# Attention masks of three batches moved from TensorE products to compare-and-multiply on VectorE

## The chip, the cores and the metric

The kernel runs on one core of one Trainium2 chip. The metric is the device time of one execution in microseconds (us); lower is better. The engines are named as in the profile: PE is TensorE's matmul, PEld its weight load, DVE is VectorE, ACT is ScalarE, POOL is GpSimd, SP issues transfers.

## The reference

Four batches, eight heads, 768 positions, head size 64. Every query and key is given to one of 16 clusters of its head; a query sees only keys of its own cluster. The result goes through a two-layer MLP with ELU.

```python
q_assign = np.argmax(np.einsum('bhsd,hcd->bhsc', q_n, c_n), axis=-1)
k_assign = np.argmax(np.einsum('bhsd,hcd->bhsc', k_n, c_n), axis=-1)
mask = q_assign[:, :, :, None] == k_assign[:, :, None, :]
scores = scale * np.matmul(q, k.transpose(0, 1, 3, 2))
scores = np.where(mask, scores, -1000000000.0)
scores = scores - np.max(scores, axis=-1, keepdims=True)
attn = np.exp(scores)
attn = attn / (np.sum(attn, axis=-1, keepdims=True) + 1e-09)
# attn @ v, then x of (3072, 512):
h = x @ w_in                                   # (512, 2048)
g = np.where(h > 0.0, h, alpha * (np.exp(np.minimum(h, 0.0)) - 1.0))
return (g @ w_out).astype(np.float32)          # (2048, 512)
```

## The kernel before

The work is cut into 48 blocks, `n` from 0 to 47. A block is one batch, one third of the queries (256 of them) and one pair of heads; `blocks` runs over batches, then thirds, then the four pairs. So a batch has twelve blocks.

`scores(n)` makes the scores of one block with the keys on the partitions. Three score tiles `s` of 128x1024 (two heads, two key tiles of 128, 256 queries) are filled in PSUM. For each key tile there is a pair of float32 products over the 64 numbers of a head (L402, the two heads on the two halves of the partitions) and a pair of bf16 products that add the mask (L411). For the mask, `hot` holds for every position a one-hot vector over the 16 clusters of the heads, with the heads on the partitions, and `qm` holds plus or minus a very large number by the query's cluster, made by `masks(n)` on ACT (L376, two instructions). Masked scores get a hugely negative term, and the exponential (L419, ACT) makes them 0 in the SBUF tile `p`. There is no maximum taken off.

`sums(n)` adds the three `p` tiles on DVE (L425 to L427), from block 10 on. `values(n)` multiplies `p` with `v` into the PSUM bank `o_bank` (L448) and makes the row sums with a product by ones into a tile `d` (L437). ACT copies both out (L462, L464), DVE takes the reciprocal (L465), POOL scales (L466). `check(n)` reads the reciprocal once more on ACT (L472).

`hidden` makes four columns' tiles of the MLP's inner layer (L487), ACT, POOL and DVE make the ELU of it (L497, L498, L504, L506, L508); the DVE part of one `hidden`, called `elu`, is issued behind the next one's products, and holds its PSUM tile until then. `outer` is the second layer: seven products (L517) into `o_bank` and `f_bank` in turn, with sums and differences of their parts on DVE and POOL (L548 to L584), so that each of the two banks is emptied before a later product writes it again.

PSUM has these two banks and a pool of three tiles `banks` of two banks each, shared by score tiles, `d`, `hidden`, transposes and similarities. `p` has three tiles.

The order is written out by hand, and every engine runs its instructions in that order. In the loop over `n` it is: `values(n-1)`, loads, `masks(n+1)`, `scores(n)`, `check(n-1)`, `sums(n)`, in blocks 8 to 11 of a batch the transposes of the next batch's q and k (L312, DVE), and then one group of MLP steps. A third's MLP has four groups, one a block: two `hidden`; two `hidden`; four products; three products. The group lies `LAG = 7` blocks behind the attention of its third, so that a batch's blocks 3, 7 and 11 have the first kind.

At a batch's last block the next batch's clusters are made between the MLP steps: `similar` multiplies with the centroids (L333) and transposes on DVE (L340); `assign` finds the largest of 16 and makes `oh` and `hot` (L350, L352, L362), and copies `hot` with its halves exchanged (L365), which the mask products of half of the heads need. The query's are behind the first `hidden`, the key's and `masks` of the next block behind the second:

```python
beside.append(None)
for j in range(2):
    beside.append(lambda b=b, j=j: [similar(b + 1, j, half) for half in range(2)])
    beside.append(lambda b=b, j=j: [assign(b + 1, j, half) for half in range(2)])
beside.append(lambda n=n: masks(n + 1))
```

In the first 176 us the MLP's weights, which arrive as 64-bit numbers, are decoded on DVE, ACT and POOL (L246 to L265), a few between the score tiles.

## Time and profile before

| | |
|---|---|
| median of 3 runs | 1054.38 us (1052.81 to 1054.87) |
| profiled execution | 1053.93 us, its span 1051.9 us |
| PE clock granted | 0.991 |
| PE busy | 1009.7 us, 96% of the span |
| DVE busy | 531.3 us, 51% |
| ACT busy | 343.2 us, 33% |
| POOL busy | 182.2 us, 17% |
| from 24 to 175 us | PE 128.58 busy, DVE 146.38 of 151.00 |
| from 467 to 710 us, twelve blocks later in the run | PE 241.57 busy, DVE 112.61 of 243.00 |

The busy time of an engine is the time in which at least one of its instructions was being worked on. PE's records overlap, so what one product costs is read from the start of one to the start of the next. In the timeline a row is the start, the duration, the engine, the line, the operation with its tiles and shapes, how many equal ones it holds, and in brackets the idle time ahead of it with what ended it. All times count from the start of the span.

### The profile page before, as it was taken

What the parts mean: (1) busy time and instruction counts of PE and PEld (TensorE: products, weight loads), DVE (VectorE), ACT (ScalarE), POOL (GpSimd) and SP (SyncE); (2) the same over time, 40 slices, a digit from 0 to 9 for tenths busy, and PEclk for the clock granted to TensorE, in tenths of its full rate; (3) what the DMA queues carried; (4) which work ended last, traced back from release to release, by engine and by line L of the source; (5) the groups of instructions that cost most, each with busy time, mean ns of one, the idle gap of its engine ahead of it and who ended that gap; (6) DMA issues with size and microseconds to landing.
All of it is one profiled execution on the core that took longest, in us unless ns stands there. A gap on an engine that the chain in (4) does not pass through costs nothing.

```text
span 1051.9 us, 14992 instructions
## 1 busy us (share of the span) xinstructions
PE 1009.7 (96%) x6403; PEld 785.7 (75%) x6403; DVE 531.3 (51%) x638; ACT 343.2 (33%) x595; POOL 182.2 (17%) x193
## 2 busy tenths in 40 slices
PE   6978997999999999999999999999999999999996
PEld 4545775778778778778877877877887787788885
DVE  4999996484344246375335325456423433433131
ACT  4665540332332242233234234223323323421010
POOL 0466654111011011011011011011011011011010
PEclk9999998999999999999999999999999999999999
DMA  9628331100122103210014012210010010100000
GB/s 306 237 89 195 107 86 31 51 16 16 50 43 49 40 27 60 51 31 17 16 45 77 20 37 59 46 36 26 21 36 17 30 36 16 31 21 1 21 1 23
DMA packets 103961, 55.60 MB, mean 53 GB/s; under 512 B 83408, under 2 KB 96720, under 8 KB 103888
## 3 DMA queue, kind: packets, MB, share of 16 engines
q1 hardware_dynamic: 103888, 54.57, 19.2%
q8 instruction: 52, 0.85, 0.4%
q14 instruction: 21, 0.17, 0.1%
HBM read 48.27 MB, written 6.29 MB: 52 GB/s over the span
## 4 chain that ended last, share of the span: by engine, by line
PE 82%; DVE 14%; ACT 2%; issue 1%; POOL 1%; DMA 0%; ACTq 0%; DVEq 0%; POOLq 0%
PE banks L487 29%; PE f_bank L517 16%; PE o_bank L517 12%; PE o_bank L448 10%; PE banks L402 9%; DVE ex L261 4%; DVE ex L246 2%; PE banks L437 2%; PE banks L411 2%; DVE r L465 1%; DVE w_out L249 1%; DVE w_in L249 1%; ACT qm L376 1%; PE banks L333 1%; ACT p L419 1%; PE banks L322 1%
## 5 line engine op out<-in xcount | busy, mean ns | idle before, releaser
L487 PE MATMUL banks<-xT,w_in 128*128 128x256 f32 x1536 | 338.4, 381 | 0.9 <-ACT p L419 0.6
L487 PEld LDWEIGHTS banks<-xT,w_in 128*128 128x128 f32 x1536 | 290.6, 190 | 47.7 <-issue 4.2
L402 PE MATMUL banks<-qT,kT 64*128 64x256 f32 x1152 | 168.2, 392 | 4.9 <-ACT p L419 4.4
L448 PE MATMUL o_bank<-p,v_raw 128*64 128x256 f32 x1152 | 144.3, 385 | 11.0 <-ACT p L419 11.0
L419 ACT ACTIVATE p<-banks 128x1024 f32<-128x1024 f32 x144 | 140.6, 1022 | 13.3 <-PE banks L411 11.8
L465 DVE RECIPROCAL r<-r 128x256 f32<-128x256 f32 x48 | 84.0, 1750 | 116.1 <-ACT r L464 116.0
L497 ACT ACTIVATE gT<-banks 128x1024 f32<-128x1024 f32 x48 | 49.1, 1023 | 277.9 <-PE banks L487 277.9
L504 DVE SCALAR_TENSOR_TENSOR gT<-gT,banks 128x1024 f32<-128x1024 f32 x48 | 58.4, 1216 | 155.1 <-POOL gT L498 155.0
L402 PEld LDWEIGHTS banks<-qT,kT 64*128 64x128 f32 x1152 | 88.7, 189 | 55.2 <-PE o_bank L448 11.1
L448 PEld LDWEIGHTS o_bank<-p,v_raw 128*64 128x64 f32 x1152 | 77.9, 137 | 64.4 <-ACT p L419 15.4
L498 POOL TENSOR_SCALAR gT<-gT 128x1024 f32<-128x1024 f32 x48 | 50.2, 1046 | 313.3 <-ACT gT L497 313.0
L466 POOL TENSOR_TENSOR xT<-xT,r 128x256 f32<-128x256 f32 x48 | 40.7, 847 | 324.5 <-DVE r L465 324.4
L517 PE MATMUL o_bank<-w_out,gT 128*128 128x256 f32 x384 | 90.7, 390 | 6.3 <-POOL w_out L298 6.3
L462 ACT COPY xT<-o_bank 128x256 f32<-128x256 f32 x48 | 17.7, 369 | 218.0 <-PE o_bank L448 218.0
L517 PEld LDWEIGHTS o_bank<-w_out,gT 128*128 128x128 f32 x384 | 73.6, 194 | 20.1 <-POOL w_out L298 7.3
L517 PE MATMUL f_bank<-w_out,gT 128*128 128x256 f32 x384 | 87.1, 380 | 1.5 <-POOL w_out L252 1.5
L411 PE MATMUL banks<-qm,hot 64*128 64x256 bf16 x576 | 80.5, 271 | 2.0 <-DVE hot L362 2.0
L517 PEld LDWEIGHTS f_bank<-w_out,gT 128*128 128x128 f32 x384 | 73.1, 191 | 11.6 <-POOL w_out L252 1.9
L425 DVE TENSOR_TENSOR psum<-p 128x1024 f32<-128x1024 f32 x38 | 46.6, 1226 | 42.2 <-ACT p L419 42.2
L376 ACT ACTIVATE qm<-hot,minus,big 64x256 bf16<-64x256 bf16 x96 | 56.7, 591 | 4.1 <-DVE hot L362 3.3
L426 DVE TENSOR_TENSOR psum<-psum,p 128x1024 f32<-128x1024 f32 x38 | 46.9, 1235 | 6.0 <-ACT p L419 3.0
L517 PE MATMUL f_bank<-w_sum,g_sum 128*128 128x256 f32 x192 | 44.7, 386 | 1.2 <-DVE part L564 1.2
(109 smaller groups left out, 859.4 us busy)
## 6 DMA issues: line engine op xcount, KB each, us to landing
v_raw<-in_v_dram SPq DMA_DIRECT2D x48, 384.0 KB, 3.2
w_sum<-in_moe_w_out_dram SPq DMA_DIRECT2D x12, 512.0 KB, 3.7
out_dram<-o_sb SPq DMA_DIRECT2D x24, 256.0 KB, 2.0
q_raw<-in_q_dram SPq DMA_DIRECT2D x48, 96.0 KB, 3.7
k_raw<-in_k_dram SPq DMA_DIRECT2D x48, 96.0 KB, 3.3
w_sum<-in_moe_w_in_dram SPq DMA_DIRECT2D x8, 512.0 KB, 6.9
w_out<-in_moe_w_in_dram SPq DMA_DIRECT2D x8, 512.0 KB, 10.2
w_out<-in_moe_w_out_dram SPq DMA_DIRECT2D x4, 512.0 KB, 4.2
```

The lines of the kernel that those rows point to most:

```text
L376: nc.scalar.activation(qm[n][rows], hot[b, 0][rows, side(pr, e), ts(third, QS)], Act.Identity, scale=m, bias=minus[rows, pr % 2 : pr % 2 + 1],
L402: nc.tensor.matmul(s[:, e, ts(m, QS)], lhsT=T[i, 1][rows, ts(kt, P)], rhs=T[i, 0][rows, cols], start=True, stop=False,)
L411: nc.tensor.matmul(s[:, e, ts(m, QS)], lhsT=hot[b, 1][rows, side(pr, e), ts(kt, P)], rhs=qm[n][rows], start=False, stop=True,)
L419: nc.scalar.activation(p, s, Act.Exp, scale=SCALE)
L426: nc.vector.tensor_tensor(to, to, pu[n, 2], op=Alu.add)
L448: nc.tensor.matmul(o_bank[64 * e : 64 * e + 64, :QS], lhsT=raw["v", n][:, e, kt], rhs=p[:, e, ts(m, QS)], start=(kt == 0), stop=(kt == NT ...
L465: nc.vector.reciprocal(r, r)
L487: nc.tensor.matmul(hf[:, f], lhsT=w_in[:, ch, ts(4 * n + f, P)], rhs=xT[b, third][:, ch], start=(ch == 0 and f % 2 == 0), stop=(ch == KC - 1),
L497: nc.scalar.activation(t, hf, Act.Exp)
L498: nc.gpsimd.tensor_scalar(t, t, 1.0, 0.0, op0=Alu.min, op1=Alu.max)
L504: nc.vector.scalar_tensor_tensor(t, t, -1.0, hf, op0=Alu.add, op1=Alu.max)
L517: nc.tensor.matmul(to[:, :QS], lhsT=left[:, f], rhs=right[:, f], start=(f == 0), stop=(f == FC // 2 - 1),)
```

## The change

In batches 2 to 4 (`b > 0`) the scores get no mask products and no `qm`. The exponential makes `p` of all scores, and behind it DVE masks `p` in place: twelve instructions a block compare the query's cluster number with the key's and multiply `p` by the outcome. `qc` holds the query's numbers as bytes, the same on every partition, for eight heads and the 256 queries of a third; `kc` holds the key's numbers, one per partition, for each key tile and head. Both are made on PE from `hot` by a product with `index16`, the number of each one-hot row, and copied out of PSUM by ACT: `key_numbers` once a batch, `query_numbers` once a third, in the place of `masks`. Batch 1 stays as it was. The one-hot `hot` has no exchanged half in batches 2 to 4; the tiles of `hot`, `oh` and `qm` share places with others or have one buffer fewer.

```diff
+    numbers = const.tile([P, NC], F32, name="numbers")
+    for n in range(NC):
+        nc.gpsimd.memset(numbers[:, n : n + 1], float(n))
+    sq = work.tile([P, H, NC], F32, name="sq", tag="r", bufs=1)
+    index = const.tile([P, H], F32, name="index")
+    nc.vector.tensor_tensor(
+        sq,
+        ident.rearrange("q (h c) -> q h c", c=NC),
+        numbers.unsqueeze(1).to_broadcast([P, H, NC]),
+        op=Alu.mult,
+    )
+    nc.vector.tensor_reduce(index, sq, axis=Axis.X, op=Alu.add)
+    index16 = const.tile([P, H], BF16, name="index16")
+    nc.vector.tensor_copy(index16, index)
...
-            hot[b, j] = route.tile([P, 2, S], BF16, name="hot", tag=f"hot{j}", bufs=1 + j)
+            hot[b, j] = route.tile([P, 2 if b == 0 else 1, S], BF16, name="hot", tag=f"hot{j}", bufs=1)
...
-        oh = route.tile([P, HS], BF16, name="oh", tag="oh", bufs=1)
+        oh = work.tile([P, HS], BF16, name="oh", tag="r", bufs=1)
...
-        for e in range(2):
+        for e in range(2 if b == 0 else 0):
             at = 64 * e
             nc.vector.tensor_copy(h[64 - at : 128 - at, 1, cols], h[at : at + 64, 0, cols])
...
+    def key_numbers(b):
+
+        ps = banks()[:, 0]
+        kc[b] = route.tile([P, NT, H], F32, name="kc", tag="kc", bufs=2)
+        for kt in range(NT):
+            nc.tensor.matmul(
+                ps[:, ts(kt, H)], lhsT=hot[b, 1][:, 0, ts(kt, P)], rhs=index16, start=True, stop=True
+            )
+        nc.scalar.copy(kc[b].rearrange("p t h -> p (t h)"), ps[:, : NT * H])
+
+    def query_numbers(b, third):
+
+        to = qc[b, third] = route.tile([P, H, QS], U8, name="qc", tag="qc", bufs=2)
+        ps = [banks() for _ in range(2)]
+        for e in range(2):
+            for pr in range(NPR):
+                rows = slice(32 * pr, 32 * pr + 32)
+                nc.tensor.matmul(
+                    ps[pr // 2][:, pr % 2, ts(e, QS)],
+                    lhsT=index16[rows, 2 * pr + e : 2 * pr + e + 1].to_broadcast([32, P]),
+                    rhs=hot[b, 0][rows, 0, ts(third, QS)],
+                    start=True,
+                    stop=True,
+                )
+        for half in range(2):
+            nc.scalar.copy(
+                to[:, 4 * half : 4 * half + 4],
+                ps[half].rearrange("p a (e n) -> p (a e) n", e=2),
+            )
+
     def masks(n):
         b, third, pr = blocks[n]
-        qm[n] = route.tile([P, QS], BF16, name="qm", tag="qm", bufs=2)
+        if b > 0:
+            if pr == 0:
+                query_numbers(b, third)
+            return
+        qm[n] = route.tile([P, QS], BF16, name="qm", tag="qc", bufs=2)
...
-                        stop=False,
+                        stop=b > 0,
                     )
-                for e in range(2):
+                for e in range(2 if b == 0 else 0):
...
             nc.scalar.activation(p, s, Act.Exp, scale=SCALE)
+            for e in range(2 if b > 0 else 0):
+                for m in range(2):
+                    nc.vector.scalar_tensor_tensor(
+                        p[:, e, ts(m, QS)],
+                        qc[b, third][:, 2 * pr + e],
+                        kc[b][:, 2 * u + m, 2 * pr + e : 2 * pr + e + 1],
+                        p[:, e, ts(m, QS)],
+                        op0=Alu.is_equal,
+                        op1=Alu.mult,
+                    )
...
+            beside.append(lambda b=b: key_numbers(b + 1))
             beside.append(lambda n=n: masks(n + 1))
```

## The prediction

> **What bounds the kernel now.** I read the page's busy shares first, then its chain, then the timeline of one block at a time. The first two say that TensorE (PE) sets the end, the third says by what step.

> ```profile
> PE 1009.7 (96%) x6403; PEld 785.7 (75%) x6403; DVE 531.3 (51%) x638; ACT 343.2 (33%) x595; POOL 182.2 (17%) x193
> PE 82%; DVE 14%; ACT 2%; issue 1%; POOL 1%; DMA 0%; ACTq 0%; DVEq 0%; POOLq 0%
> L411 PE MATMUL banks<-qm,hot 64*128 64x256 bf16 x576 | 80.5, 271 | 2.0 <-DVE hot L362 2.0
> ```

> The chain's 14% of VectorE (DVE) lies in its first 176 us, where the weights are decoded. The change puts no mask there: its masks begin with batch 2, at 467 us. From 176 us on PE follows PE. The L411 row is a trap: 80.5 us busy for 576 mask products looks like 60 us in the three batches concerned. The timeline gives their real step. This is PE in one block, which I call a D block (its MLP group holds the last three products):

> ```profile
> 511.91 0.60 PE L437 MATMUL banks<-psum,ones 128*64 128x256 f32 x4
> 512.45 0.70 PE L402 MATMUL banks<-qT,kT 64*128 64x256 f32 x4
> 512.98 0.28 PE L411 MATMUL banks<-qm,hot 64*128 64x256 bf16 x2
> 513.09 0.60 PE L402 MATMUL banks<-qT,kT 64*128 64x256 f32 x4
> 513.53 0.28 PE L411 MATMUL banks<-qm,hot 64*128 64x256 bf16 x2
> ...
> 515.90 3.72 PE L517 MATMUL f_bank<-w_sum,g_sum 128*128 128x256 f32 x16
> 519.46 3.62 PE L517 MATMUL o_bank<-w_sum,gT 128*128 128x256 f32 x16
> 522.91 3.62 PE L517 MATMUL f_bank<-w_out,gT 128*128 128x256 f32 x16
> ```

> From start to start a score pair takes 0.44 us and a mask pair 0.11 (512.98 to 513.09). VectorE in the same block:

> ```profile
> 513.13 1.75 DVE L465 RECIPROCAL r<-r 128x256 f32<-128x256 f32 x1 [3.25 <-ACT r L464]
> 516.19 1.23 DVE L425 TENSOR_TENSOR psum<-p 128x1024 f32<-128x1024 f32 x1 [1.30 <-ACT p L419]
> 517.52 1.23 DVE L426 TENSOR_TENSOR psum<-psum,p 128x1024 f32<-128x1024 f32 x1
> 518.77 0.69 DVE L427 TENSOR_TENSOR psum<-psum 128x512 f32<-128x512 f32 x1
> 519.66 0.42 DVE L570 TENSOR_TENSOR o_sb<-f_bank,part 128x256 f32<-128x256 f32 x1 [0.20 <-PE f_bank L517]
> ```

> L570 empties f_bank, and the third product (522.91) writes f_bank again: L570 has only 2.8 us to spare. VectorE is half idle, but its order is fixed, and this is the place where that counts.

> [...] L554 at 582.32 is recorded with 0.42 us, and L555 behind it starts at 582.66, 0.34 later. [...] L300 took 3.24 us beside POOL's L298, where the equal L299 took 1.23. [...]

> **The change, part by part.** V is the start of a block's row sums (L437). Before, the MLP group starts at V+3.99 in kinds A, C and D (529.10 to 533.09, 571.06 to 575.05, 511.91 to 515.90) and at V+4.66 in B (549.74 to 554.40). MLP groups: A hidden 0 and 1, B hidden 2 and 3, C four products, D three. Batches 2 to 4 have 36 blocks: three first ones (n = 12, 24, 36), six other B, and nine each of C, D and A.

> 1. Mask products gone. Six pairs of 0.11: 0.65 us a block, so the group starts at V+3.35. In B one bank pair is held by a pending elu; only two go round, and the third score tile waits for the first exponential (before: 0.40 us idle at 553.12). L376, 2 x 0.6 us on ScalarE (ACT), stood ahead of that exponential and is gone: score tile 3 can start at V+2.55, the group at V+3.6. Gain 1.05 in B. Six B: +6.3; nine C: +5.85; nine D: +5.85; three A without new products (n = 23, 35, 47): +1.95.

> 2. Masks on VectorE: 12 a block, 432 in all, 128x256 with a per-partition scalar. The trace has no such row. Below, 0.34 (the step above); above, 0.42, the whole recorded time of a 256-element instruction, no overlap. The pointer may add: L191 (64 elements, with pointer) took 251 ns, L178 (without) 224. I take 0.38. They stand behind the reciprocal, whose end also releases POOL's L466 (723 ns at least, reads SBUF): once a block it locks out a mask for about 0.7. Masks therefore take 12x0.38+0.7 = 5.3 us, V+2.95 to V+8.2. VectorE's total, 531 us and 432x0.38 = 164, stays far below the span; only its lateness counts.
>    - D: the sums take 3.27 (516.19 to 519.46) and end at V+11.5, L570 behind them (0.42) at V+11.9. The third product wants f_bank at V+10.35: 3.35, and 3.55 and 3.45 for the two products ahead of it. Stall 1.55, in seven D blocks; in two (n = 22, 34) the transposes L312 (1.83) stand between too: 3.4. Sum 17.7.
>    - C: an elu delays the reciprocal's end to V+3.2; sums, L549 (1.14) and L554 (0.34) then free f_bank at V+13.25, the fourth product wants it at V+13.8 (three products of 3.45 behind V+3.35): hidden. With transposes (n = 21, 33) V+15.1: 1.3 each, 2.6.
>    - A at n = 23, 35: masks, sums and transposes hold VectorE until V+13.3, then L340 (0.58) empties the query's first similarity at V+13.9. Hidden 1 needs that bank and would be ready at V+11.9 (3.35, hidden 0 of 7.1, similarities of 1.43): 2.0 each, 4.1 for both.
>    - B: elu follows at V+13.4; hidden 3 ends only at V+17.6, and its bank comes from an exponential. Hidden; without that cover the C block's first scores would wait.

> 3. Key numbers, three times, behind the key's similarities. Before, PE went on with L448 at once (467.19), and VectorE's last transposes of hot came 4 us later:

> ```profile
> 465.76 1.50 PE L333 MATMUL banks<-kT,cT 128*32 128x384 f32 x16
> 467.19 2.81 PE L448 MATMUL o_bank<-p,v_raw 128*64 128x256 f32 x24
> 471.33 0.58 DVE L362 STREAM_TRANSPOSE hot<-oh 128x384 bf16<-128x384 bf16 x1
> ```

>    Now PE waits for that transpose. Without one half's copies (L365, 0.54) it ends at 471.25; six small products, the copy of kc, which the second query bank waits for, and eight query products end at about 472.25: values 5.05 late. Behind PE's wait are values, row sums and scores. The scores then run as in B, without the present stall: 1.05 back. Net 4.0 each, 12.0. Not shown in the trace: small products, from nothing to 0.1 each (a 64x128 bf16 weight load is 95 ns).

> 4. Query numbers ahead of six A blocks (n = 15, 19, 27, 31, 39, 43). PE's eight products, at most 8 x 0.11, hide under ACT's reading of the row sums (until V+1.18). Then ACT copies twice 128x1024 (as L497: 1.02). Score tiles 2 and 3 wait for those copies, the third until V+3.25; the group starts at V+4.25. Loss 0.25 each, 1.5. If bytes are written more slowly or quickly, 0 to 0.6 each.

> 5. Prologue: 16 memsets on POOL (L919's stand 0.035 apart, L216 takes 0.10: 0.6 to 1.6 together), then three instructions on VectorE ahead of cen, 0.29+0.29+0.16. The chain runs through cen (0.75 to 5.66): loss 0.8, from 0 to 1.7. The shared tags of oh, qc and hot cost nothing: their last readers end blocks earlier, and the second oh is behind the first on the same engine. No DMA is added, and SP's queue keeps its order.

> Sum: gains 6.3+5.85+5.85+1.95 = 19.95; losses 17.7+2.6+4.1+12.0+1.5+0.8 = 38.7. Net 18.7 slower. The profiled execution took 1053.93 us (span 1051.9); that gives 1072.6. The median of three, 1054.38, is 0.45 above it.

> **Rivals.**
> - Cheap masks: 0.34 each and no lock. D then stalls 0.34 seven times and 2.2 twice (6.8), C 0.2, L340 1.7: 3 slower, 1057. For it: POOL gets its 0.7 in an idle gap today. Against: the gap (1.30) is filled.
> - Faster: the D wait vanishes. It decides at 12 masks by V+6.3, which with the lock means 0.25 us a mask. Then only step 3, 4 and 5 remain against 19.95: 5.65 faster, 1048.3. Against: below the shortest 256-element step in the trace.
> - Full serial masks at 0.44 or above: D 2.3 and 4.1, C late in all blocks, L340 2.8: about 30 slower, 1083. For it: in-place writes; against: no wait stands between the four of a tile in the built order.
> - The change does not do what it says: nothing gained on PE, if mask pairs ran beside the scores all along. The 0.54 steps of 0.44 + 0.11 speak against it; it would give 1090.

> **How the numbers follow.** Forecast 0.72, cheap masks 0.13, faster 0.05, serial masks or no gain 0.10. A measurement of this kernel tells 0.2% (2.1 us) from no change. Faster by more: 0.06, with a tail of the cheap case. Within: 0.06, the cheap case with a short key wait. Slower: 0.88. The forecast's own bounds are 0.34 to 0.42 a mask (6 either way) and 1 us on each key wait: 1062 to 1083. Reaching for the cheap case and a part of the serial one: 1056 to 1086.

> **What would show it.** L411 down to 144 pieces; PE gaps at the third D product released by L570, about 1.5 us; a gap of 4 us behind L333 released by hot, three times; mask rows with starts 0.38 apart and one hole of 0.7; POOL L466 longer than 0.73. It is wrong if the third D product starts without a gap, if the key gap is below 2 us, or if masks start under 0.3 apart.

## The result, and the profile after

The changed kernel takes 1082.33 us (median of four runs, 1079.81 to 1083.55), against 1054.43 for the kernel before beside it: a ratio of 1.0264, 95% interval 1.0242 to 1.0287. The profiled execution took 1081.51 us, of which 1078.0 are its span; the forecast was 1072.6, with a range from 1056 to 1086. The direction was right, and the size was short by 9 to 10 us.

Busy time, chain and the row of the masks, from the page of the kernel after:

```profile
PE 1006.2 (93%) x6061; PEld 780.7 (72%) x6061; DVE 705.8 (65%) x1049; ACT 316.7 (29%) x544; POOL 182.6 (17%) x209
PE 69%; DVE 25%; ACT 2%; issue 2%; POOL 0%; DVEq 0%; ACTq 0%; POOLq 0%
L472 DVE SCALAR_TENSOR_TENSOR p<-qc,kc,p 128x256 f32<-128x256 uint8 x432 | 185.4, 501 | 5.9 <-ACT p L469 5.9
```

PE lost 342 products and only 3.5 us of busy time. VectorE gained 174.5 us of work and is still busy for only 65% of the span, yet its share of the chain rose from 14% to 25%. So VectorE is not full; it is late in certain places. The timeline shows where. PE in a D block (block 26), where in the kernel after L452 are the scores and L577 the products of the second layer:

```profile
528.67 0.60 PE L497 MATMUL banks<-psum,ones 128*64 128x256 f32 x4
529.20 2.86 PE L452 MATMUL banks<-qT,kT 64*128 64x256 f32 x24
531.99 3.72 PE L577 MATMUL f_bank<-w_sum,g_sum 128*128 128x256 f32 x16
535.55 3.62 PE L577 MATMUL o_bank<-w_sum,gT 128*128 128x256 f32 x16
540.28 3.72 PE L577 MATMUL f_bank<-w_out,gT 128*128 128x256 f32 x16 [1.11 <-DVE o_sb L630]
```

and VectorE in the same block:

```profile
529.89 1.75 DVE L525 RECIPROCAL r<-r 128x256 f32<-128x256 f32 x1 [3.25 <-ACT r L524]
531.56 5.21 DVE L472 SCALAR_TENSOR_TENSOR p<-qc,kc,p 128x256 f32<-128x256 uint8 x12
536.69 1.21 DVE L485 TENSOR_TENSOR psum<-p 128x1024 f32<-128x1024 f32 x1
...
539.20 0.69 DVE L487 TENSOR_TENSOR psum<-psum 128x512 f32<-128x512 f32 x1
539.81 0.42 DVE L630 TENSOR_TENSOR o_sb<-f_bank,part 128x256 f32<-128x256 f32 x1
```

Before, the first product began 3.99 us behind the row sums; here it is 3.32 (528.67 to 531.99). But twelve masks now stand ahead of the three sums, and L630, which empties f_bank, starts at 539.81. Before, the third product began 3.45 us behind the second (519.46 to 522.91, in the prediction's lines). Here it begins 4.73 behind it: it is 1.28 us late, of which the trace calls 1.11 a gap. Behind this gap the product also takes 0.10 longer until the next work starts (3.65 instead of 3.55). Together this is a stall of 1.38, and the block, which has gained 0.67 on its scores, ends 0.71 later than before.

PE at the end of batch 2, where the next batch's key numbers are made (L349 the key's similarities, L391 the key numbers, L403 the query numbers, L508 the values):

```profile
477.52 1.50 PE L349 MATMUL banks<-kT,cT 128*32 128x384 f32 x16
481.38 0.23 PE L391 MATMUL banks<-index,hot 128*128 128x8 bf16 x3 [2.36 <-DVE hot L378]
483.02 0.23 PE L391 MATMUL banks<-index,hot 128*128 128x8 bf16 x3 [1.42 <-DVE hot L378]
483.19 0.75 PE L403 MATMUL banks<-hot,index 32*128 32x256 bf16 x8
483.86 4.50 PE L508 MATMUL o_bank<-p,v_raw 128*64 128x256 f32 x24
```

Before, the values followed the similarities 1.43 us behind their start (465.76 to 467.19); now 6.34. And the values themselves, 24 products that took 2.81 us in every block from n = 11 on in the kernel before, take 4.50. The trace gives the clock granted to PE (the column PEclk, 1.00 for full speed) in three stretches around them:

```profile
core 0: us, PE busy (x) PEld busy (x) DVE busy (x) ACT busy (x) POOL busy (x), PEclk, DMA share, GB/s
480.65:484.06 3.41, 1.19 (x16) 0.68 (x18) 2.21 (x7) 0.38 (x2) 0.00 (x0) 1.00 0.00 0
484.06:487.47 3.41, 3.41 (x18) 1.96 (x16) 0.00 (x0) 1.75 (x2) 0.00 (x0) 0.50 0.03 5
487.47:490.88 3.41, 3.25 (x28) 2.04 (x24) 1.48 (x1) 1.82 (x5) 0.00 (x0) 1.00 0.35 99
```

Behind the two gaps PE has half its clock for 3.41 us, which is 0.5 x 3.41 = 1.7 us of work lost, the same as 4.50 less 2.81. The same happens in the two D blocks with transposes (n = 22 and 34). In n = 22:

```profile
448.77 5.41 PE L577 MATMUL f_bank<-w_out,gT 128*128 128x256 f32 x16 [2.83 <-DVE o_sb L630]
```

16 products that take 3.72 take 5.41 behind a gap of 2.83 us. Behind the gap of 1.11 in block 26 they took 3.72. This lowered clock is what the prediction did not have.

The whole difference, block by block, each from the start of its values to the start of the next block's, kernel after against kernel before, with the forecast's own terms:

| place | count | forecast, each | measured, each |
|---|---|---|---|
| until the start of block 11 | 1 | +0.8 | +1.46 |
| last block of a batch, n = 11 | 1 | +5.05 | +5.14 |
| last block of a batch, n = 23, 35 | 2 | +6.45 | +5.90 |
| first block of a batch, n = 12, 24, 36 | 3 | -1.05 | +0.92, +0.75, +0.75 |
| D | 7 | +0.90 | +0.71 |
| D with transposes, n = 22, 34 | 2 | +2.75 | +4.12 |
| C | 7 | -0.65 | -0.67 |
| C with transposes, n = 21, 33 | 2 | +0.65 | +0.41 |
| A with query numbers | 6 | +0.25 | +0.13 |
| A without, n = 47 | 1 | -0.65 | -0.67 |
| B | 6 | -1.05 | -0.81 |
| sum | | +18.7 | +25.4 |

The measured sum is the delay of the last values; the span is 26.1 longer.

### The profile page after: what moved, and what is told of

Its sections match the earlier page's. It is cut to its first block, busy times and chain, and to the rows that moved or that the text cites. A ratio compares the mean times of both kernels' runs of the same rounds, so it can differ in the third digit from the quotient of the medians.

```text
span 1078.0 us, 14694 instructions
## 1 busy us (share of the span) xinstructions
PE 1006.2 (93%) x6061; PEld 780.7 (72%) x6061; DVE 705.8 (65%) x1049; ACT 316.7 (29%) x544; POOL 182.6 (17%) x209
## 4 chain that ended last, share of the span: by engine, by line
PE 69%; DVE 25%; ACT 2%; issue 2%; POOL 0%; DVEq 0%; ACTq 0%; POOLq 0%
PE banks L547 29%; PE f_bank L577 12%; PE o_bank L508 11%; PE o_bank L577 7%; PE banks L452 6%; DVE p L472 6%; DVE r L525 3%; DVE ex L277 3%; PE banks L497 2%; DVE ex L262 2%; DVE psum L486 1%; DVE psum L485 1%; DVE w_in L265 1%; PE banks L349 1%; ACT p L469 1%
## 5 line engine op out<-in xcount | busy, mean ns | idle before, releaser
L472 DVE SCALAR_TENSOR_TENSOR p<-qc,kc,p 128x256 f32<-128x256 uint8 x432 | 185.4, 501 | 5.9 <-ACT p L469 5.9
L508 PE MATMUL o_bank<-p,v_raw 128*64 128x256 f32 x1152 | 151.5, 400 | 11.1 <-ACT p L469 11.1
L452 PE MATMUL banks<-qT,kT 64*128 64x256 f32 x1152 | 147.8, 388 | 4.8 <-ACT p L469 2.7
L469 ACT ACTIVATE p<-banks 128x1024 f32<-128x1024 f32 x144 | 140.1, 1025 | 23.1 <-PE banks L452 18.7
L452 PEld LDWEIGHTS banks<-qT,kT 64*128 64x128 f32 x1152 | 100.8, 187 | 43.8 <-PE o_bank L508 9.0
L508 PEld LDWEIGHTS o_bank<-p,v_raw 128*64 128x64 f32 x1152 | 81.1, 142 | 67.0 <-issue 19.6
L577 PE MATMUL f_bank<-w_out,gT 128*128 128x256 f32 x384 | 91.6, 393 | 15.6 <-DVE o_sb L630 13.5
L526 POOL TENSOR_TENSOR xT<-xT,r 128x256 f32<-128x256 f32 x48 | 39.6, 825 | 337.6 <-DVE r L525 337.6
L577 PEld LDWEIGHTS f_bank<-w_out,gT 128*128 128x128 f32 x384 | 74.4, 196 | 30.4 <-DVE o_sb L630 17.1
L577 PE MATMUL o_bank<-w_out,gT 128*128 128x256 f32 x384 | 90.5, 389 | 6.2 <-POOL w_out L314 6.2
L577 PEld LDWEIGHTS o_bank<-w_out,gT 128*128 128x128 f32 x384 | 73.2, 193 | 20.3 <-POOL w_out L314 7.3
L577 PE MATMUL f_bank<-w_sum,gT 128*128 128x256 f32 x192 | 44.8, 387 | 1.7 <-DVE o_sb L614 1.6
L577 PE MATMUL f_bank<-w_sum,g_sum 128*128 128x256 f32 x192 | 44.6, 386 | 1.2 <-DVE part L624 1.2
```

The lines of the kernel that those rows point to most:

```text
L452: nc.tensor.matmul(s[:, e, ts(m, QS)], lhsT=T[i, 1][rows, ts(kt, P)], rhs=T[i, 0][rows, cols], start=True, stop=b > 0,)
L469: nc.scalar.activation(p, s, Act.Exp, scale=SCALE)
L472: nc.vector.scalar_tensor_tensor(p[:, e, ts(m, QS)], qc[b, third][:, 2 * pr + e], kc[b][:, 2 * u + m, 2 * pr + e : 2 * pr + e + 1], p[:, e ...
L508: nc.tensor.matmul(o_bank[64 * e : 64 * e + 64, :QS], lhsT=raw["v", n][:, e, kt], rhs=p[:, e, ts(m, QS)], start=(kt == 0), stop=(kt == NT ...
L577: nc.tensor.matmul(to[:, :QS], lhsT=left[:, f], rhs=right[:, f], start=(f == 0), stop=(f == FC // 2 - 1),)
```

## The experiments

Two theories stood against each other. **Waits:** the loss is PE's waiting for VectorE, in the D blocks and at the batch ends, and each wait costs what the timeline shows of it. **Waits and clock:** besides that, PE runs slowly for a few us behind a long gap, which costs 1.7 us at five places. The rival that the masks' sheer volume costs the time is tested by two runs: one leaves the masks out, another keeps them all and changes only the order on VectorE.

**Key numbers behind the values.** The key numbers are not made in the last MLP group, where PE must wait for VectorE's last transpose, but behind the next block's values and row sums.

```diff
             values(n - 1)
+            if 0 < b < B and at == 0:
+                key_numbers(b)
...
-            beside.append(lambda b=b: key_numbers(b + 1))
```

> The changed kernel, with the key numbers made one step later: behind values(n-1) of the next batch's first block instead of ahead of it. Theory (PE waits in order for the key's clusters, 5.1 us three times, and then runs at a lower granted clock for about 3.5 us, 1.7 us three times): values need nothing of the clusters and cover most of the wait. The gap behind the similarities falls from 3.8 us to under 1.5 us, values take 2.8 us again instead of 4.5, and each batch end costs 0 to 1 us against the kernel before instead of 6: about 16 us less than the changed kernel, 1064 to 1068. Rival (the loss lies in VectorE's masks alone, the wait is only shifted to the scores): within 3 us of the changed kernel, 1079 to 1083.

Measured: 1066.88 us (1064.54 to 1067.81), 1.0113 of before (1.0093 to 1.0133). The last blocks now cost +1.10, +2.09 and +2.09, and each first block behind them gains 0.24 to 0.25 where it had lost 0.75 to 0.92. PE at the end of batch 2:

```profile
473.80 1.50 PE L349 MATMUL banks<-kT,cT 128*32 128x384 f32 x16
475.35 0.28 PE L403 MATMUL banks<-hot,index 32*128 32x256 bf16 x2
476.00 0.39 PE L403 MATMUL banks<-hot,index 32*128 32x256 bf16 x6 [0.36 <-DVE sim L356]
476.32 2.81 PE L508 MATMUL o_bank<-p,v_raw 128*64 128x256 f32 x24
```

The wait for hot is gone, and the values take 2.81 again. The place of six tiny products a batch costs 15 us in three batches. This run can't part the wait from the clock, as it removes both.

**Masks left out.**

```diff
-            for e in range(2 if b > 0 else 0):
+            for e in range(0):
                 for m in range(2):
                     nc.vector.scalar_tensor_tensor(
```

> The changed kernel without the 432 mask instructions on VectorE; the mask is left out in batches 2 to 4, numbers of clusters are still made. Theory: all stalls by late masks go (seven times 1.4, twice 4.8 with the clock's part, twice 1.1 and twice 1.4: 24 us), the waits at the batch ends stay: 1056 to 1060, PE gaps behind the similarities unchanged. Rival (the batch ends and the query copies are the loss, the masks hide): 1076 or more. Other rival (masks are all of it): 1048 or less.

Measured: 1055.33 (1054.04 to 1056.69), ratio 1.001 (1.0001 to 1.0019). All C and D blocks now gain 0.67, with or without transposes. The batch ends stay: +4.91 at n = 11, +4.24 at 23 and 35, +0.75 in the block behind, and the values there again take 4.50. So the masks are guilty of the D and C delays, and of 1.66 us in each of the last blocks n = 23 and 35, which cost 5.90 with masks; the rest of the batch ends is not theirs. With 432 masks gone and the one-hot products gone too, the kernel is still no faster than before. Compared with the run further down that has no mask at all, the batch ends and the blocks behind them use up 19.8 us of the gain, and the query numbers in six A blocks 4.8.

**The wait filled, first try.** Eight float32 products that nobody reads are put between the steps of the last group, to keep PE busy through the gap.

```diff
+    def fill():
+        for _ in range(8):
+            nc.tensor.matmul(o_bank[:, :QS], lhsT=cT, rhs=w_in[:, 0, :QS], start=True, stop=True)
...
+            beside.append(fill)
             beside.append(lambda b=b: key_numbers(b + 1))
```

> The changed kernel with eight float32 products of 128x128 by 128x256 into o_bank put behind the key's similarities, where PE stands idle; their result is overwritten. They take 3.5 us and the clusters come 4 us later. Theory (values behind the gap are slow because PE's granted clock falls in a gap of 4 us): values take 2.8 us instead of 4.5, three times 1.7: 5 us less, 1076 to 1078, although PE has more to do. Rival (values are slow there since ACT copies the query numbers or weights are fetched at that time): values stay at 4.5 us and the time at 1081 to 1083. Other rival (the gap is not waiting for VectorE): 10 us longer.

Measured: 1084.17 (1082.57 to 1084.21), ratio 1.0279 (1.0262 to 1.0296): a miss, and not a clean one. The longer list of steps was spread anew over the group; the key's similarities came ahead of the second hidden, which then waited 2.99 us for L356. The values did take 2.81, and the block behind gained 0.94, but the total says nothing.

**The wait filled, second try.** The same eight products, in one step with the key numbers and directly ahead of them, so that nothing else moves:

```diff
-            beside.append(lambda b=b: key_numbers(b + 1))
+            beside.append(lambda b=b: [fill(), key_numbers(b + 1)])
```

> The changed kernel with eight float32 products of 128x128 by 128x256 into o_bank directly ahead of the key numbers' products, where PE stands idle; their result is overwritten, and everything else keeps its place (in the filled kernel before, the list of steps grew by one and the key's similarities slipped ahead of the second hidden). Theory (values behind the gap are slow because PE's granted clock falls in a gap of about 4 us): values take 2.8 us at all three batch ends instead of 4.5, about 5 us less than the changed kernel: 1075 to 1079, although PE has more to do. Rival (values are slow because of ACT's copies or other work at that time): values stay at 4.5 us, 1080 to 1084.

PE at the end of batch 2 in this kernel (L664 are the filling products):

```profile
471.13 1.50 PE L349 MATMUL banks<-kT,cT 128*32 128x384 f32 x16
472.56 3.72 PE L664 MATMUL o_bank<-w_in,cT 128*128 128x256 f32 x16
476.11 0.22 PE L391 MATMUL banks<-index,hot 128*128 128x8 bf16 x3
476.63 0.23 PE L391 MATMUL banks<-index,hot 128*128 128x8 bf16 x3 [0.30 <-DVE hot L378]
477.47 2.81 PE L508 MATMUL o_bank<-p,v_raw 128*64 128x256 f32 x24
```

The values start 6.34 us behind the similarities' start, exactly as in the kernel after: the same hot ends the same wait. But PE was busy meanwhile, and the values take 2.81. The last blocks n = 23 and 35 cost +5.91 and +5.90 as in the kernel after, n = 11 costs +4.91 instead of +5.14 (there the clock had already fallen ahead of the values), and the blocks behind the three gain 0.94 each where they had lost 0.92, 0.75 and 0.75: 1.86 + 1.69 + 1.69 = 5.2 us saved by products whose result is thrown away. That parts the clock from the wait. The total, 1070.27 (1069.69 to 1073.76), ratio 1.0161 (1.0139 to 1.0183), is lower than expected, and not all that was saved belongs to the filling. Of the 11.8 us between the two profiled executions 5.4 do (with the 0.2 at n = 11), 2.6 came in the decoding stage, whose code is the same, 1.5 lie outside the span, and 1.7 came in block 22, where the filling isn't:

```profile
444.06 3.72 PE L577 MATMUL f_bank<-w_out,gT 128*128 128x256 f32 x16 [2.83 <-DVE o_sb L630]
```

This is the product that took 5.41 in the kernel after, behind the same gap of 2.83. Block 34 of the same run had +4.13 again, the slow product. So a gap of 2.83 us can cost 1.7 us or nothing. What parts the two shows in stretches of 3.41 us, the length of a fall of the clock. The ones for block 34 are laid so that one ends where the clock falls; the ones for block 22 lie 73 such lengths of 3.413 earlier (694.71 less 445.54 is 249.17). The columns are those of the table of stretches above:

```profile
442.12:445.54 3.42, 1.48 (x7) 1.32 (x8) 2.31 (x4) 0.00 (x0) 0.73 (x1) 1.00 0.00 0
445.54:448.95 3.41, 3.41 (x23) 2.51 (x23) 0.42 (x1) 0.00 (x0) 0.62 (x1) 1.00 0.00 0
691.29:694.71 3.42, 1.41 (x7) 1.26 (x8) 2.38 (x4) 0.00 (x0) 0.73 (x1) 1.00 0.01 2
694.71:698.12 3.41, 3.41 (x10) 2.69 (x9) 0.00 (x0) 0.00 (x0) 0.00 (x0) 0.50 0.01 2
```

The same gap lies a little differently across these stretches. In block 22 PE is busy for 1.48 us of the stretch ahead and keeps its clock; in block 34 it is busy for 1.41 and loses half of it. The last section takes this further.

**Sums behind a step.** The sums of C and D blocks, and the transposes behind them, are issued behind the group's second (C) or first (D) product, so that the emptying of f_bank comes ahead of them on VectorE; in the last block of a batch the transposes stay ahead and the sums follow the first step.

```diff
-            if n >= LAG + 3:
-                sums(n)
+            def rest_of_block(n=n, b=b, at=at, ahead=ahead):
+                if n >= LAG + 3:
+                    sums(n)
...
+            late = {1: 2, 2: 1}.get(n % 4, 0) if b > 0 else 0
...
+            if not late:
+                rest_of_block()
...
+            if n < len(blocks) and late == m + 1:
+                rest_of_block()
```

> The changed kernel with another order on VectorE in batches 2 to 4: in C blocks sums and transposes stand behind the group's second product, in D blocks behind its first, and in a batch's last block the transposes go ahead of the sums and the sums behind the query's clusters. No work is added or taken away. Theory (L630 and L614 empty f_bank late, because masks push them; 3.3 us of sums and 1.8 of transposes need not be ahead of them): D gaps of 1.3 and 2.8 us and the C gap go, 20 us less: 1060 to 1064. Rival (VectorE is short of time, so that an order that helps one wait makes the next): 1076 to 1083, with a new wait for the sums at L497 or for the second o_bank sum.

Measured: 1058.3 (1057.14 to 1059.46), ratio 1.0042 (1.0026 to 1.0059). VectorE in the same D block as above:

```profile
520.67 5.21 DVE L472 SCALAR_TENSOR_TENSOR p<-qc,kc,p 128x256 f32<-128x256 uint8 x12
525.81 0.41 DVE L630 TENSOR_TENSOR o_sb<-f_bank,part 128x256 f32<-128x256 f32 x1
526.14 1.21 DVE L485 TENSOR_TENSOR psum<-p 128x1024 f32<-128x1024 f32 x1
```

The masks take as long as in the kernel after, but L630 no longer stands behind the sums, and all D and C blocks, also n = 21, 22, 33 and 34, gain 0.67. The batch ends stay in the main (+4.91, +4.95, +5.05). The spans differ by 25.0 us, more than expected: 21.4 in the C and D blocks, the slow clock of n = 22 and 34 included, nearly 3 at the batch ends, 0.8 in the first stage, whose code is the same. Leaving all masks out shortened the span by 25.8, so it is nearly all the order on VectorE that costs time here, not the amount of its work.

**Both moves together.** The edits of the first and the last experiment in one kernel.

> The key numbers behind values, as in the first experiment, and VectorE's order with the sums behind a product, as in the fourth. If the two losses are separate the savings add: 15.4 and 24.0 us off the changed kernel's 1082.3 give 1042.9, range 1040 to 1046, faster than the kernel before. Rival (both remove the same idle time, or the key numbers now wait for the sums): 1050 or more.

Measured: 1042.82 (1042.02 to 1045.9), ratio 0.99 (0.9879 to 0.992). D and C gain 0.67 each, the last blocks cost 1.02 to 1.09, the first ones gain 0.25. The savings add up as forecast, so the two losses are separate. The masks on VectorE are worth having, if nothing waits for them.

**No mask at all.** The kernel before, without `qm` and without the mask products in batches 2 to 4, and with nothing on VectorE:

```diff
-                        stop=False,
+                        stop=b > 0,
...
-                for e in range(2):
+                for e in range(2 if b == 0 else 0):
```

> The kernel before without the mask products (L411) and without qm (L376) in batches 2 to 4: the mask is left out there, nothing takes its place. Measures the gain on PE by itself. Theory by the trace of the changed kernel (0.67 us a block, 0.81 in B blocks): 27 x 0.67 + 9 x 0.81 = 25.4 us less than the kernel before: 1027 to 1031. If mask pairs cost what their busy time says (60 us): 995. If they run beside the scores: 1050 or more.

Measured: 1029.33 (1026.62 to 1031.42), ratio 0.9758 (0.9734 to 0.9782). Each A, C and D block gains 0.66 to 0.68, each B 0.80 to 0.82, each first block 0.93 to 0.95. The gain that the prediction put on PE is real, block by block, and some 25 us is the most that taking the mask off PE and ACT can bring in this order of the work.

**Query numbers between the products.** The kernel with both moves, and the query numbers of a batch's second and third third made behind the first product of the D block instead of ahead of the A block's scores.

```diff
-            if pr == 0:
+            if pr == 0 and third == 0:
                 query_numbers(b, third)
...
+            if b > 0 and n < len(blocks) and n % 4 == 2 and m == 0 and at + 2 < NB:
+                query_numbers(b, at // NPR + 1)
```

> As the kernel with both moved, and the query numbers of a batch's second and third third made behind the first product of a D block, where no score tile is waiting for a PSUM tile, instead of ahead of an A block's scores. Theory (an A block loses 0.13 us instead of gaining 0.67, because its score tiles wait for the copies; PE's own eight products take 0.4): six times 0.4 us, 2 to 4 us less than the kernel with both moved. Rival (the copies only move the wait): the same within 1 us.

Measured: 1040.97 (1040.65 to 1041.49), ratio 0.9871 (0.9855 to 0.9888), 1.9 us below the kernel with both moves. The A blocks gain 0.67 instead of losing 0.13, and the D blocks give 0.53 of that back (0.14 gained instead of 0.67). It is the fastest version that masks by number, 1.3% faster than before.

## Why the prediction was right or wrong

**In sum.** The direction, the waits and what ends them were right in the main; one cost was missing, the slow clock behind long waits. That the measured time still fell inside the stated range was luck: its upper end was room for slower masks, and the clock was not in it.

**What bounds the kernel, and step 1: right.** PE's gain stood at 0.65 for A, C and D; the runs show 0.67. In B it was 1.05 against 0.81. The third score tile starts 2.79 us behind the row sums, not 2.55: I had let L376 go and the first exponential start as soon as ACT was free, but it then waits for its own scores.

**Step 2: right in mechanism and nearly in size.** Twelve masks and POOL's hole: 5.3 forecast, 5.13 measured (531.56 to 536.69). In blocks where POOL does not meet them they take 4.76, 0.40 each; I took 0.38. The 0.34 of L554, the prediction's lower bound, was too low: L554 reads PSUM and has no number per partition, and so was not the same case. The meeting with POOL's L526 then costs about 0.37, where I had put 0.7, the whole of POOL's instruction; so the two sizes erred in opposite directions. That 0.7 was an estimate from L300, which took 3.24 us beside POOL's L298; L299 is recorded beside L298 too (164.93 to 166.16 us, L298 from 165.04) and took its 1.23. A hold is seen here: the second mask of block 26 is recorded with 0.95 us instead of 0.47 and ends 0.28 behind the end of L526, which took 0.81 instead of 0.73. But the row of masks loses only half of POOL's time by it, 0.37 of 0.73. The D stall was 1.38 against 1.55, C with transposes 1.08 against 1.3, and the predicted releaser, the emptying of f_bank, stands in the bracket. In the last blocks n = 23 and 35 the masks cost 1.66 against 2.0, in part by a wait that I had not seen: PE stops for 0.89 us inside the query's similarities, for the transpose of q (L328) that they read, before it comes to the forecast wait for their own transpose (L340, now L356).

**D with transposes: the wait right, its price wrong.** Forecast 3.4. The wait was 3.1 (the product starts 6.45 behind the one ahead of it instead of 3.45, and takes the same 0.10 more as in the other D blocks), but behind it the product ran 1.69 longer. Two places, 3.4 us.

**Step 3: the wait right, its return wrong.** "Values 5.05 late" was 4.91 (6.34 less 1.43) at n = 23 and 35, and 5.14 at n = 11, where the clock had fallen before the values began. "The scores then run as in B: 1.05 back" is where the sum failed: the return is there, 0.94 with the gap filled, but 1.69 to 1.86 us of slow clock came on top. Three places, 5.2 us.

So the missed term of the sum is 3.4 + 5.2 = 8.6 us, at five places. The rest of the steps together came out 1.2 us below forecast within the span, which makes 18.7 + 8.6 - 1.2 = 26.1. I had checked each wait for what stands behind it on the engine, and took what stands there at its old duration. The trace of the kernel after has the price: a clock of 0.50 for 3.41 us, half of which is 1.7. Which gaps had it is taken up below.

**Step 4** cost 0.13 instead of 0.25. **Step 5** can't be read: at the start of block 11 the kernel after stands at +1.46, but kernels with the same code until there stand between -1.17 and +3.18, so this stage varies by more than the 0.8 that I had put.

**The rivals.** Masks at 0.34 or at 0.44 are both out (0.40), and "faster" needed 0.25. The total alone would not have told: full serial masks were put at 1083, next to the 1082.3 measured, but with D stalls of 2.3 and a delay in every C block, and neither is there. That nothing would be gained on PE is refuted by the run with no mask at all.

**Open.** 1.5 us of the profiled difference lie outside the span: 2.0 us there before, 3.5 after. The kernels with the key numbers behind the values or with the sums moved have 3.5 to 4.3 too, the one with masks left out and the two with filling 1.8 to 2.2. No edit that I can name goes with it.

## What to carry to other kernels

Here a new wait of PE had two prices: the wait, and slow products behind it, about 1.7 us at each of five places, where PE had been busy for only 1.14 to 1.39 of the 3.41 us ahead of the fall of its clock. The filled wait and the gaps of 1.11 and 0.89 us had only the first. When work moves to a half idle engine, look at the order in which that engine issues it: here the same masks made the kernel 2.6% slower, or only 0.4% slower once the sums no longer stood ahead of the instruction that PE waits for. A small product that needs a late result belongs behind work that doesn't need it: with the key numbers moved as well the kernel was 1.0% faster than before, and with the query numbers moved too 1.3%.
